# Two loads in place of one for the preceding rows of the first chunk, and a new order of the steps

## The chip, the cores and the metric

The kernel runs on one core of a Trainium2 chip. The metric is the device time of one execution in microseconds (us); lower is better. A core has TensorE (PE in the profile, its weight loads PEld), VectorE (DVE), ScalarE (ACT), GpSimd (POOL) and SyncE (SP), each with its own stream of instructions that it works off in order, and 16 DMA engines. A difference of about 0.3% between two versions is what their repeated times can tell from none.

## The reference

The input x has 8 sequences of 4160 rows of 192 numbers; each row has 8 heads with 7 taps each. The first half is a short causal attention: the taps of a head go through a softmax, and each row becomes the weighted sum of itself and the six rows ahead of it in its sequence (zeros ahead of the first).

```python
w = np.exp(weight_gen - np.max(weight_gen, axis=-1, keepdims=True))
w = w / (np.sum(w, axis=-1, keepdims=True) + 1e-09)
x_pad = zeros(B, 6, D) followed by x;  x_unf = x_pad[:, s + k]  (k = 0..6)
out = np.einsum('bshk,bskhg->bshg', w, x_unf)
```

The second half takes the 33280 rows of the result as tokens:

```python
h = x @ w_in                                   # 192 -> 1024
sm = exp(h - max(h)) / (sum(...) + 1e-09)
solu = h * sm
ln = (solu - mean) / sqrt(var + 1e-06) * g_ln
return ln @ w_out                              # 1024 -> 192
```

All of it is float32 in and out.

## The kernel before, in words

The 33280 rows are cut into 128 runs of 260 consecutive rows, one run for each partition; a sequence is 16 partitions. A tile t is row t of all 128 runs, so there are 260 tiles. They are loaded in chunks: tiles 0 to 3, 4 to 11, 12 to 19, and then 15 chunks of 16 tiles. A chunk's buffer `xt` holds the chunk's rows and the six rows ahead of them (`HALO`); there are two such buffers, and three for the taps `wt`.

For the first chunk the six rows ahead of a run are the last six rows of the run before, that is of the partition before. Line 73 loads the four rows of the chunk on all 128 partitions, line 74 clears the six rows of partition 0, and line 75 loads the last six rows of runs 0 to 126 to partitions 1 to 127. Step `x0` (line 243) then zeroes these rows where a partition begins a sequence. The second chunk takes its six rows from the first one's buffer (line 81, step `x1`); all later chunks are loaded with their six rows in four parts (`lx0` to `lx3`, line 85), the taps in one (`lw`, line 91).

The steps of a chunk, with their names in the planner: the squares of x are summed for a scale (`v00` to `v03`, ACT, line 143; then `v1` to `v5`, lines 149 to 167); the softmax of the taps is `t0` (maximum, DVE, line 107), `t1` (subtraction, POOL, line 109), `t2` (exponential, ACT, line 113), `t3` (sum, DVE, line 115), `t4` (ACT, line 118, which needs the scale from `v2`), `t5` (reciprocal, DVE, line 120) and `t6` (multiplication, POOL, line 122). Then POOL multiplies and adds for groups of four tiles (two in the first chunk): `attA` (line 178) and `attB` (lines 189 to 194); `fin` (DVE, line 469) and `dup` (ACT, line 479) finish a group.

The steps of a tile: `xT` transposes two tiles on PE (line 493), `xhi` and `xld` split them in two float16 parts (lines 501, 507), `mm1` is the first product (PE, lines 519 and 522), then `max` (DVE, 534), `exp` (ACT, 540), `solu` (DVE, 548), `sq` (ACT, 554), `hi` (ACT, 561), `lo` (DVE, 565), `tr` (a transposing DMA from SP's queue, 573), `mm2` (the second product, PE, 613), `out` (ACT, 624, which empties the accumulator `po` and so lets the next `mm2` start) and `od` (the store, 627). `f0` to `f5` are small steps on the statistics of up to four tiles (lines 588 to 604).

At the start the weights are loaded and split into two parts each (`a..`, `b..`, `c..`, `q..`, `n..`, `p..`, lines 251 to 413): raw_a and raw_b are w_in (line 207 from ACT's queue, line 208 from SP's, into the buffer named `hl`), raw_2 is w_out (line 214, into the buffer named `wide`).

What stands in which order on an engine is set in the program by a planner. `plan` lists all steps with engine, cost in ns, the steps that they wait for and an earliest time; `issue_order` plays the list through: each engine takes, among its steps whose predecessors are over, the one with the smallest key, which is the tile's number plus the step's entry in `URGENCY`. The order that comes out is the order of emission, written out under a manual schedule. The planner's times are used for nothing else; on the chip an instruction waits for what it reads, wherever it stands.

Of the kernel before, what the change touches and what calls it, by code (L numbers as in the profile page):

```python
# [26 lines left out]
def tile_kernel(ctx: ExitStack, tc: tile.TileContext, x, weight_gen, w_in, w_out, g_ln, out):  # L27
    nc = tc.nc
    P = 128
# [6 lines left out]
    HALO = K - 1  # L36
    RUN = B * S // P
    PB = P // B
# [17 lines left out]
    x_run = x.rearrange("b (q t) d -> (b q) t d", t=RUN)  # L56
# [8 lines left out]
    def load_x(c, part=0):  # L65
        t0, n = starts[c], starts[c + 1] - starts[c]
        if part == 0:
            xs[c] = io.tile([P, (TC + HALO) * D], F32, name="xt")
        xt = xs[c]
        xv = xt.rearrange("p (t d) -> p t d", d=D)  # L70
        if c == 0:

            nc.sync.dma_start(xv[:, HALO : HALO + n, :], x_run[:, :n, :])
            nc.vector.memset(xt[:1, : HALO * D], 0.0)
            nc.sync.dma_start(xv[1:, :HALO, :], x_run[: P - 1, RUN - HALO :, :])
        elif t0 < HALO:
            if part == 0:
                nc.sync.dma_start(xv[:, HALO : HALO + n, :], x_run[:, t0 : t0 + n, :])
            else:
                first = xs[0].rearrange("p (t d) -> p t d", d=D)  # L80
                nc.sync.dma_start(xv[:, :HALO, :], first[:, t0 : t0 + HALO, :])
        else:
            cuts = [(HALO + n) * k // LOADS for k in range(LOADS + 1)]
            r0, r1 = cuts[part], cuts[part + 1]
            nc.sync.dma_start(xv[:, r0:r1, :], x_run[:, t0 - HALO + r0 : t0 - HALO + r1, :])
# [146 lines left out]
    sq = const.tile([P, 8], F32, name="sq")  # L232
# [402 lines left out]
    def at_chunk(op, *args):  # L635
# [3 lines left out]
        attA=attend, attB=add_up, fin=last_sum, dup=copy_columns, xT=transpose_x,  # L639
        xhi=high_x, xld=low_x, mm1=first_product,  # L640
        max=maximum, exp=exponentials, solu=solu, sq=squares, hi=high_half, lo=low_half,
# [37 lines left out]


URGENCY = dict(
    a00=11.1, a01=-98.4, a02=25.1, a03=-179.2, a04=-48.9, a10=186.8, a11=18, a12=-184.5, a13=64.6,
    a14=-6.8, attA=76.8, attB=48.3, b0=-43.3, b1=-63.8, b2=-61.6, b3=198.8, b4=12.7, c00=62.4,
    c01=-82.8, c02=-0, c10=-111.1, c11=170.7, c12=56.5, c20=5.9, c21=34.4, c22=-3.9, c30=95.7,
    c31=-78.4, c32=-191, dup=40.3, exp=-27.1, f0=110.8, f1=-58.2, f2=-34.4, f3=-54.9, f4=15.4,
    f5=7.4, fin=13.5, hi=48.7, lo=-241.4, lw=10, lx0=53.1, lx1=133.3, lx2=75.6, lx3=108.2, max=88,
    mm1=-12.9, mm2=-6, n0=-189.5, n1=236.9, n2=-43.5, n3=-30.3, n4=153, n5=186, n6=-45.4, n7=-79.4,
    od=-11, out=-36.3, p30=-216.9, p31=16.6, p4=69.6, p5=143.5, p6=44.6, p70=154.1, p71=155.3,
    p80=127.5, p81=5.7, q00=-151, q01=12.5, q02=-55, q10=97.5, q11=-186.5, q12=108.7, q20=50,
    q21=178.6, q22=151.1, q30=-31.4, q31=-114, q32=237.3, solu=-1.8, sq=68, t0=134.4, t1=-160.3,  # L690
    t2=44.1, t3=-111, t4=-150.2, t5=-33.5, t6=245.4, tr=13.9, v00=221, v01=162, v02=94.7, v03=234.3,
    v1=-130.7, v2=160, v3=1, v4=87.6, v5=29.8, x0=-119.5, x1=-81.8, xT=-15.1, xhi=45.2, xld=182.9,
)


# [4 lines left out]
def plan(run, starts, group, stat_group, loads, parts):  # L700

    PE, DVE, ACT, SP, POOL = range(5)
    steps = []

    def add(name, t, engine, cost, *after, ready=0):
        steps.append((name, t, engine, cost, [x for x in after if x[1] >= 0], ready))

    def once(name, engine, cost, *after, ready=0):
        add(name, 0, engine, cost, *((x, 0) for x in after), ready=ready)
# [1 line left out]
    def chunk_of(t):  # L711
        return max(c for c in range(len(starts) - 1) if starts[c] <= t)

    weights = dict(a0=7000, a1=8500, b=9300, c0=13000, c1=14500, c2=15000)
    order = list(weights)
    norm_of = dict(a0="n0", a1="n1", b="n2")
    for n, part in enumerate(order):
# [28 lines left out]
    for half in "01":  # L746
        once("p7" + half, ACT, 826, "p3" + half, "p4")
        once("p8" + half, DVE, 929, "p7" + half)
    once("x0", DVE, 1200, "v00", ready=6000)
    once("x1", SP, 2500, "x0")  # L750

    def last_group(c):
# [9 lines left out]
    for c in range(len(starts) - 1):  # L762
        t, before = starts[c], starts[c - 1] if c > 1 else -1
        size = starts[c + 1] - t
        whole = size == 16
        if c > 1:
            add("lw", t, SP, 1270, last_group(c - 3))
            add("lx0", t, SP, 1540, last_group(c - 2), *parts_of(c - 2))
            for n in range(1, loads):
                add(f"lx{n}", t, SP, 1540, (f"lx{n - 1}", t))  # L770
        for part in range(4 if whole else 1):
            if c > 1:
                load = min(part + 1, loads - 1) if whole else loads - 1
                add(f"v0{part}", t, ACT, 840 if whole else 1600, (f"lx{load}", t))
            else:
                add(f"v0{part}", t, ACT, (2000, 1600)[c], ready=18000 if c else 6000)
        add("v1", t, DVE, 74, *parts_of(c), *parts_of(c - 1), ("f5", starts[c - 4] - 1 if c > 4 else -1))
        add("v2", t, ACT, 940, ("v1", t))
        add("v3", t, ACT, 480, ("v2", t), ("n6", 0))
        add("v4", t, DVE, 76, ("v3", t))  # L780
        add("v5", t, ACT, 190, ("v4", t))
        n = size * 8
        wide = 60 + 7.35 * n
        on = (DVE, POOL, ACT, DVE, ACT, DVE, POOL)
        costs = (wide, 13.4 * n, 100 + 5.9 * n, wide, 260 + n, 60 + 6.3 * n, 13.4 * n)
        for k in range(7) if c else range(4, 7):
            after = [(f"t{k - 1}", t)] if k and (c or k > 4) else []
            if k == 4:
                after.append(("v2", t))
            if k == 0 and c > 1:  # L790
                after += [("lw", t), ("t6", before)]
            add(f"t{k}", t, on[k], costs[k], *after, ready=10500 if c == 1 and not k else 0)
# [87 lines left out]
    return steps  # L880


def issue_order(steps):

    PE, DVE, ACT, SP, POOL = range(5)
    SAME, CROSS, FROM_PE = (25, 127, 143, 0, 102), 130, 200
    free = [2000, 5000, 4500, 6500, 4500]
    number = {(name, t): i for i, (name, t, *_) in enumerate(steps)}
    then, count, ready = [[] for _ in steps], [0] * len(steps), [s[5] for s in steps]
    for i, step in enumerate(steps):  # L890
        for x in step[4]:
            then[number[x]].append(i)
            count[i] += 1
    key = [round(t + URGENCY.get(name, 0), 6) for name, t, *_ in steps]
    later, now = [[] for _ in free], [[] for _ in free]
    for i, step in enumerate(steps):
        if not count[i]:
            heapq.heappush(later[step[2]], (ready[i], key[i], i))

    def gap(e, to):  # L900
        if e == to and to != SP:
            return SAME[e]
        return FROM_PE if e == PE and to != SP else CROSS

    queue = data = 0
    busy = warm = -10000
    order = []
    while True:
        able = [
            (free[e] if now[e] else max(free[e], later[e][0][0]), e)  # L910
            for e in range(len(free)) if now[e] or later[e]
        ]
        if not able:
            break
        time, e = min(able)
        while later[e] and later[e][0][0] <= time:
            _, k, i = heapq.heappop(later[e])
            heapq.heappush(now[e], (k, i))
        k, i = heapq.heappop(now[e])
        if ready[i] > time:  # L920
            heapq.heappush(later[e], (ready[i], k, i))
            continue
        name, t, _, cost, *_ = steps[i]
        order.append((name, t))
        free[e] = end = time + cost
        if e == PE:

            if name != "xT" and time - busy > 2000:
                warm = time + 3400
            if time < warm:  # L930
                free[e] = end = time + 2 * cost if time + 2 * cost < warm else (time + warm) / 2 + cost
            if name != "xT":
                busy = end
        if e == SP:
            queue = max(queue, time) + (625 if name == "tr" else 450)
            data = max(queue + 650, data) + cost
            free[e], end = time + 60, data + 950

        if name in ("sq", "lo"):
            j = number["lo" if name == "sq" else "sq", t]  # L940
            ready[j] = max(ready[j], end + CROSS)
        for j in then[i]:
            ready[j] = max(ready[j], end + gap(e, steps[j][2]))
            count[j] -= 1
            if not count[j]:
                heapq.heappush(later[steps[j][2]], (ready[j], key[j], j))
    assert len(order) == len(steps)
    return order
# [33 lines left out]
```

## Time and profile before

| | |
|---|---|
| time, median of 3 runs | 1330.26 us (1329.93 to 1333.56) |
| profiled execution | 1328.66 us, its span 1326.9 us |
| busy PE, DVE, ACT, POOL | 1212.0, 1166.0, 1179.7, 1187.2 us |
| mean granted TensorE clock | 0.993 of full speed |
| read from HBM, written | 46.19 MB, 25.56 MB |

A line of the profile names line, engine and operation, what is written and read by the program's tile names, and times in us. A wait is given as the idle time of an engine ahead of an instruction with what ended it. Matmuls are pipelined and their ends are modelled, so a busy PE is not PE at its peak; spans on POOL are rough. The profile holds one execution.

### The profile page before, as it was taken

How to read it: one execution, taken by the hardware profiler on the slowest of the kernel's cores; microseconds unless marked ns; L12 is line 12 of the kernel's file. 1: busy time of each engine (PE TensorE's matmuls, PEld its weight loads, DVE VectorE, ACT ScalarE, POOL GpSimd, SP SyncE). 2: the span in 40 equal slices, each digit the busy share in tenths (PEclk: the TensorE clock that was granted, in tenths of full speed). 3: DMA queues.
4: the chain of work that ended last, by engine and by line, in shares of the span. 5: the costliest groups of instructions: out<-in, count | busy, mean ns of one | idle time of the engine just before them, and what ended most of it. 6: DMA issues, size and time to landing. Idle time of an engine off the chain costs nothing.

```text
span 1326.9 us, 27167 instructions
## 1 busy us (share of the span) xinstructions
PE 1212.0 (91%) x10428; PEld 835.8 (63%) x10428; DVE 1166.0 (88%) x1800; ACT 1179.7 (89%) x2366; POOL 1187.2 (89%) x241
## 2 busy tenths in 40 slices
PE   0468898998999999999999999999999999999998
PEld 0245565665766666666666666666666666676666
DVE  1788898989989899998989899898989999899995
ACT  0679898999989899999999899999989999899886
POOL 0899999998999999999999999999999999999920
PEclk9979999999999999999999999999999999999999
DMA  4357779787786978688787968779697867877776
GB/s 131 108 125 167 157 132 206 144 180 151 159 183 132 204 145 185 143 171 183 135 199 149 211 129 181 159 158 193 133 206 140 191 138 157 178 143 127 128 152 129
DMA packets 565203, 210.44 MB, mean 159 GB/s; under 512 B 544337, under 2 KB 545745, under 8 KB 565072
## 3 DMA queue, kind: packets, MB, share of 16 engines
q1 hardware_dynamic: 564784, 207.64, 75.2%
q8 instruction: 82, 1.34, 0.4%
q10 hardware_dynamic: 288, 1.05, 0.2%
q14 instruction: 49, 0.40, 0.1%
HBM read 46.19 MB, written 25.56 MB: 54 GB/s over the span
## 4 chain that ended last, share of the span: by engine, by line
PE 57%; ACT 15%; DMA 11%; issue 5%; DVE 5%; POOL 4%; SPq 1%; ACTq 0%; DVEq 0%; POOLq 0%
PE po L613 25%; PE h L522 18%; DMA xt<-in_x_dram 11%; PE h L519 10%; PE pa L493 5%; ACT e L540 4%; ACT hl L561 4%; ACT e L554 4%; DVE hl L565 2%; POOL pr L178 2%; SPq L573 1%; DVE h L534 1%; ACT ot L624 1%; DVE h L548 1%; ACT x_hi L501 1%
## 5 line engine op out<-in xcount | busy, mean ns | idle before, releaser
L178 POOL TENSOR_TENSOR pr<-xt,wt 128x5376 f32<-128x5376 f32 (+1 forms) x66 | 630.9, 9558 | 3.9
L613 PE MATMUL po<-w_hl,hlT 128*128 128x192 f16 x6192 | 554.4, 246 | 33.9 <-ACT ot L624 33.9
L613 PEld LDWEIGHTS <-hlT 128*128 128x128 f16 x6240 | 523.7, 98 | 73.7 <-issue 38.9
L565 DVE SCALAR_TENSOR_TENSOR hl<-h,hl 128x1024 f16<-128x1024 f32 x260 | 315.6, 1220 | 63.9 <-ACT hl L561 32.1
L548 DVE SCALAR_TENSOR_TENSOR h<-h,row,e 128x1024 f32<-128x1024 f32 x260 | 333.2, 1282 | 36.9 <-ACT e L540 34.9
L534 DVE TENSOR_SCALAR_CACHE_REDUCE h<-h,row 128x1024 f32<-128x1024 f32 x260 | 334.4, 1286 | 11.9 <-PE h L522 10.4
L540 ACT ACTIVATE e<-h,stats 128x1024 f32<-128x1024 f32 x260 | 293.3, 1128 | 9.4 <-DVE h L534 8.1
L554 ACT ACTIVATE e<-h,stats 128x1024 f32<-128x1024 f32 x260 | 291.8, 1122 | 3.9 <-DVE hl L565 3.0
L561 ACT ACTIVATE hl<-h 128x1024 f16<-128x1024 f32 x260 | 267.4, 1028 | 28.9 <-DVE stats L585 19.4
L522 PE MATMUL h<-wa_hi,x_hi 128*128 128x512 f16 x520 | 200.7, 386 | 0.0
L522 PE MATMUL h<-wa_lo,x_hi 128*128 128x512 f16 x520 | 198.1, 381 | 0.0
L522 PE MATMUL h<-wa_hi,x_lo 128*128 128x512 f16 x520 | 198.1, 381 | 0.0
L522 PEld LDWEIGHTS <-x_hi 128*128 128x128 f16 x1040 | 80.6, 98 | 173.1 <-issue 112.2
L189 POOL TENSOR_TENSOR wide<-pr 128x2304 f32<-128x2304 f32 (+1 forms) x34 | 167.6, 4929 | 2.3
L192 POOL TENSOR_TENSOR pr<-pr 128x2304 f32<-128x2304 f32 x32 | 162.3, 5072 | 1.5
L143 ACT ACTIVATE junk<-xt 128x768 f32<-128x768 f32 (+2 forms) x63 | 56.5, 897 | 69.2 <-DMA xt<-in_x_dram 69.2
L519 PE MATMUL h<-wb_hi,x_hi 64*128 64x512 f16 x520 | 102.0, 388 | 15.5 <-ACT e L554 12.6
L624 ACT ACTIVATE ot<-po,stats 128x192 f32<-128x192 f32 x258 | 111.1, 431 | 4.0 <-PE po L613 3.6
L194 POOL TENSOR_TENSOR half<-pr 128x1536 f32<-128x1536 f32 x32 | 110.4, 3449 | 2.5
L493 PE MATMUL pa<-ident,wide 128*128 128x128 f32 x792 | 99.1, 275 | 1.6 <-DVE x_lo L507 1.1
L519 PE MATMUL h<-wb_lo,x_hi 64*128 64x512 f16 x520 | 99.7, 379 | 0.0
L519 PE MATMUL h<-wb_hi,x_lo 64*128 64x512 f16 x520 | 99.6, 378 | 0.1
(97 smaller groups left out, 1141.7 us busy)
## 6 DMA issues: line engine op xcount, KB each, us to landing
out_dram<-ot SPq DMA_DIRECT2D x65, 384.0 KB, 2.7
xt<-in_x_dram SPq DMA_DIRECT2D x30, 576.0 KB, 4.7
xt<-in_x_dram SPq DMA_DIRECT2D x30, 480.0 KB, 4.6
wt<-in_weight_gen_dram SPq DMA_DIRECT2D x15, 448.0 KB, 3.7
hlT<-hl SPq DMA_TRANSPOSE x260, 4.5
wide<-in_moe_w_out_dram SPq DMA_DIRECT2D x2, 768.0 KB, 20.6
xt<-in_x_dram SPq DMA_DIRECT2D x3, 384.0 KB, 5.2
raw_a<-in_moe_w_in_dram ACTq DMA_DIRECT2D x2, 512.0 KB, 5.9
```

Of the source, the lines that this page charges most:

```text
L178: nc.gpsimd.tensor_tensor(out=window(pr, 0, [(TG * D, K), (HG, n * H), (1, HG)]), in0=window(xt, t * D, [(D, K), (HG, n * H), (1, HG)]), i ...
L189: nc.gpsimd.tensor_tensor(out=out, in0=pr[:, :3], in1=pr[:, 3:6], op=ALU.add)
L493: nc.tensor.matmul(pa[:, n, i, :], source, ident, is_transpose=True, start=at == 0, stop=at == len(terms) - 1,)
L519: nc.tensor.matmul(h[:, fs], lhs[rows, 1, :], rhs[rows], start=n == 0, stop=False)
L522: nc.tensor.matmul(h[:, fs], lhs[:, 0, :], rhs[:, fs], start=False, stop=n == 2)
L534: nc.vector.tensor_scalar(h, h, row(t, BACK), 3.0e38, op0=ALU.mult, op1=ALU.min, accum_out=stat(t, NMAX))
L540: nc.scalar.activation(e, h_of[t], AF.Exp, bias=stat(t, NMAX), scale=-1.0, accum_out=stat(t, Z))
L548: nc.vector.scalar_tensor_tensor(out=h, in0=h, scalar=row(t, SCALE), in1=e, op0=ALU.mult, op1=ALU.mult, accum_out=stat(t, M))
L554: nc.scalar.activation(e_of.pop(t), h_of[t], AF.Square, bias=stat(t, M), scale=-float(FF), accum_out=stat(t, Q),)
L561: nc.scalar.activation(hl[:, 0, :], h_of[t], AF.Copy, scale=2.0**14)
L565: nc.vector.scalar_tensor_tensor(out=hl[:, 1, :], in0=h_of[t], scalar=2.0**14, in1=hl[:, 0, :], op0=ALU.mult, op1=ALU.subtract,)
L613: nc.tensor.matmul(po[:, :D], hlT[:, half * NJ + j, :], w2_hl[:, j, w, :], start=n == 0, stop=n == len(terms) - 1,)
```

## The change

The load of the six preceding rows of the first chunk (127 partitions) becomes two loads, of 112 and of 15 partitions, from the same place to the same place. In the planner the earliest times of the weight steps a0, a1 and b, of the first squares and of `x0`, and the cost of `x0`, are other numbers; a table `MARGIN` adds 3 or 6 us to the time between certain steps of tiles from 12 on (a name's first two letters are looked up: `lx` to `v0`, `lw` to `t0`, `lx` to `at`, and so on); and nearly all entries of `URGENCY` are new. No other instruction is added or taken away.

```diff
--- before.py
+++ after.py
@@ -72,7 +72,8 @@
 
             nc.sync.dma_start(xv[:, HALO : HALO + n, :], x_run[:, :n, :])
             nc.vector.memset(xt[:1, : HALO * D], 0.0)
-            nc.sync.dma_start(xv[1:, :HALO, :], x_run[: P - 1, RUN - HALO :, :])
+            for p0, p1 in ((1, 1 + P - PB), (1 + P - PB, P)):
+                nc.sync.dma_start(xv[p0:p1, :HALO, :], x_run[p0 - 1 : p1 - 1, RUN - HALO :, :])
         elif t0 < HALO:
             if part == 0:
                 nc.sync.dma_start(xv[:, HALO : HALO + n, :], x_run[:, t0 : t0 + n, :])
@@ -679,17 +680,18 @@
 
 
 URGENCY = dict(
-    a00=11.1, a01=-98.4, a02=25.1, a03=-179.2, a04=-48.9, a10=186.8, a11=18, a12=-184.5, a13=64.6,
-    a14=-6.8, attA=76.8, attB=48.3, b0=-43.3, b1=-63.8, b2=-61.6, b3=198.8, b4=12.7, c00=62.4,
-    c01=-82.8, c02=-0, c10=-111.1, c11=170.7, c12=56.5, c20=5.9, c21=34.4, c22=-3.9, c30=95.7,
-    c31=-78.4, c32=-191, dup=40.3, exp=-27.1, f0=110.8, f1=-58.2, f2=-34.4, f3=-54.9, f4=15.4,
-    f5=7.4, fin=13.5, hi=48.7, lo=-241.4, lw=10, lx0=53.1, lx1=133.3, lx2=75.6, lx3=108.2, max=88,
-    mm1=-12.9, mm2=-6, n0=-189.5, n1=236.9, n2=-43.5, n3=-30.3, n4=153, n5=186, n6=-45.4, n7=-79.4,
-    od=-11, out=-36.3, p30=-216.9, p31=16.6, p4=69.6, p5=143.5, p6=44.6, p70=154.1, p71=155.3,
-    p80=127.5, p81=5.7, q00=-151, q01=12.5, q02=-55, q10=97.5, q11=-186.5, q12=108.7, q20=50,
-    q21=178.6, q22=151.1, q30=-31.4, q31=-114, q32=237.3, solu=-1.8, sq=68, t0=134.4, t1=-160.3,
-    t2=44.1, t3=-111, t4=-150.2, t5=-33.5, t6=245.4, tr=13.9, v00=221, v01=162, v02=94.7, v03=234.3,
-    v1=-130.7, v2=160, v3=1, v4=87.6, v5=29.8, x0=-119.5, x1=-81.8, xT=-15.1, xhi=45.2, xld=182.9,
+    a00=-75.5, a01=196.4, a02=120, a03=-176, a04=47.5, a10=-10.6, a11=207.7, a12=103.2, a13=184.6,
+    a14=20.7, attA=-120.3, attB=-79, b0=164.4, b1=-62.4, b2=-50.4, b3=-19.9, b4=-4.1, c00=-70.9,
+    c01=120.7, c02=38.6, c10=39.6, c11=-101.6, c12=161.2, c20=147.6, c21=248.5, c22=-170.5,
+    c30=95.7, c31=-78.4, c32=-191, dup=-95.9, exp=47.3, f0=163.9, f1=-43, f2=68.5, f3=-25.1,
+    f4=-119.5, f5=-175.5, fin=178.2, hi=-75, lo=-86.8, lw=74.8, lx0=49.7, lx1=-160.2, lx2=-51.3,
+    lx3=-50.1, max=79.2, mm1=-17.5, mm2=-11.1, n0=-238.4, n1=155.8, n2=-86.8, n3=-42.6, n4=-198.3,
+    n5=149.2, n6=168.1, n7=40.5, od=-47, out=-56.3, p30=-80.9, p31=228.3, p4=51.3, p5=19.5, p6=80.1,
+    p70=225.4, p71=-108.2, p80=105.2, p81=3.6, q00=-6.6, q01=11.4, q02=150.6, q10=29.9, q11=-8.3,
+    q12=-71.5, q20=71.7, q21=44.1, q22=6.6, q30=-30.5, q31=172.3, q32=-17.3, solu=-18.3, sq=73,
+    t0=-244.2, t1=161.4, t2=-209.3, t3=175.5, t4=57.9, t5=-91.9, t6=76, tr=-50.4, v00=50.7, v01=-70,
+    v02=36.1, v03=156.4, v1=-183.3, v2=247.2, v3=131.1, v4=191.5, v5=-81.1, x0=110.7, x1=-165.6,
+    xT=-20.3, xhi=-169.3, xld=158.9,
 )
 
 
@@ -711,7 +713,7 @@
     def chunk_of(t):
         return max(c for c in range(len(starts) - 1) if starts[c] <= t)
 
-    weights = dict(a0=7000, a1=8500, b=9300, c0=13000, c1=14500, c2=15000)
+    weights = dict(a0=5700, a1=7000, b=9000, c0=13000, c1=14500, c2=15000)
     order = list(weights)
     norm_of = dict(a0="n0", a1="n1", b="n2")
     for n, part in enumerate(order):
@@ -746,7 +748,7 @@
     for half in "01":
         once("p7" + half, ACT, 826, "p3" + half, "p4")
         once("p8" + half, DVE, 929, "p7" + half)
-    once("x0", DVE, 1200, "v00", ready=6000)
+    once("x0", DVE, 820, "v00", ready=6500)
     once("x1", SP, 2500, "x0")
 
     def last_group(c):
@@ -773,7 +775,7 @@
                 load = min(part + 1, loads - 1) if whole else loads - 1
                 add(f"v0{part}", t, ACT, 840 if whole else 1600, (f"lx{load}", t))
             else:
-                add(f"v0{part}", t, ACT, (2000, 1600)[c], ready=18000 if c else 6000)
+                add(f"v0{part}", t, ACT, (2000, 1600)[c], ready=18000 if c else 6500)
         add("v1", t, DVE, 74, *parts_of(c), *parts_of(c - 1), ("f5", starts[c - 4] - 1 if c > 4 else -1))
         add("v2", t, ACT, 940, ("v1", t))
         add("v3", t, ACT, 480, ("v2", t), ("n6", 0))
@@ -880,6 +882,13 @@
     return steps
 
 
+MARGIN = {
+    ("lx", "v0"): 6000, ("lw", "t0"): 6000, ("lx", "at"): 6000, ("t0", "t1"): 6000,
+    ("t1", "t2"): 3000, ("t2", "t3"): 3000, ("t3", "t4"): 3000, ("v2", "t4"): 3000,
+    ("t5", "t6"): 6000,
+}
+
+
 def issue_order(steps):
 
     PE, DVE, ACT, SP, POOL = range(5)
@@ -897,10 +906,12 @@
         if not count[i]:
             heapq.heappush(later[step[2]], (ready[i], key[i], i))
 
-    def gap(e, to):
-        if e == to and to != SP:
-            return SAME[e]
-        return FROM_PE if e == PE and to != SP else CROSS
+    def gap(step, to):
+        e, on = step[2], to[2]
+        late = MARGIN.get((step[0][:2], to[0][:2]), 0) if to[1] > 11 else 0
+        if e == on and on != SP:
+            return SAME[e] + late
+        return (FROM_PE if e == PE and on != SP else CROSS) + late
 
     queue = data = 0
     busy = warm = -10000
@@ -940,7 +951,7 @@
             j = number["lo" if name == "sq" else "sq", t]
             ready[j] = max(ready[j], end + CROSS)
         for j in then[i]:
-            ready[j] = max(ready[j], end + gap(e, steps[j][2]))
+            ready[j] = max(ready[j], end + gap(steps[i], steps[j]))
             count[j] -= 1
             if not count[j]:
                 heapq.heappush(later[steps[j][2]], (ready[j], key[j], j))
```

## Prediction

> **What bounds the kernel now.** I read the page's chain of waits first. Its lines name TensorE (PE) for 57% of the span and a load of x for 11%, which is much for a kernel that loads ahead.
>
> ```profile
> span 1326.9 us, 27167 instructions
> PE 1212.0 (91%) x10428; PEld 835.8 (63%) x10428; DVE 1166.0 (88%) x1800; ACT 1179.7 (89%) x2366; POOL 1187.2 (89%) x241
> PE 57%; ACT 15%; DMA 11%; issue 5%; DVE 5%; POOL 4%; SPq 1%; ACTq 0%; DVEq 0%; POOLq 0%
> ```
>
> Four engines are busy for 88 to 91% of the span, so a stall of one has little room to be made up by another. Next I read the chain in order of time, and the timeline of the first 60 us, where the span is emptiest.
>
> ```profile
> 1.65 31.55 DMA xt<-in_x_dram
> ...
> 1.19 0.42 SPq L73 DMA_DIRECT2D xt<-in_x_dram  x1
> 1.65 0.32 SPq L75 DMA_DIRECT2D xt<-in_x_dram  x1
> 2.02 13.62 SPq L208 DMA_DIRECT2D hl<-in_moe_w_in_dram  x2
> 33.31 1.80 ACT L143 ACTIVATE junk<-xt 128x1920 f32<-128x1920 f32 x1 [31.30 <-DMA xt<-in_x_dram]
> 35.24 0.16 DVE L149 TENSOR_REDUCE row<-squares_x 128x1 f32<-128x8 f32 x1 [27.41 <-ACT junk L143]
> 38.40 0.57 POOL L122 TENSOR_TENSOR wt<-wt,wy 128x224 f32<-128x224 f32 x1 [32.17 <-DMA xt<-in_x_dram]
> 42.20 0.67 ACT L270 ACTIVATE size<-wide 128x512 f32<-128x512 f32 x1 [3.73 <-DVE h L274]
> 57.94 0.61 PE L519 MATMUL h<-wb_hi,x_hi 64*128 64x512 f16 x2
> ```
>
> The load of line 75 (the preceding rows of the first chunk) is issued at 1.65 us and is back at 33.20 us. ACT's first instruction on data waits for it, DVE's line 149 waits for ACT, POOL's line 122 for what follows from that: the three engines stand still together. The second column of these rows is a duration; the brackets hold the idle time before the row. The first product of the main loop starts at 57.94 us. The same stretch by windows (columns: window, its length, busy time and count of PE, PEld, DVE, ACT, POOL, clock, DMA share, GB/s) and the sizes of the loads (KB each, median us from issue to landing) tell why:
>
> ```profile
> 2.00:4.00 2.00, 0.00 (x0) 0.00 (x0) 0.29 (x4) 0.01 (x1) 0.00 (x0) 1.00 0.82 210
> 4.00:6.00 2.00, 0.00 (x0) 0.00 (x0) 0.71 (x2) 0.00 (x0) 0.59 (x2) 1.00 0.98 354
> 6.00:8.00 2.00, 0.00 (x0) 0.00 (x0) 1.76 (x3) 0.00 (x0) 0.23 (x1) 1.00 0.55 221
> 8.00:10.00 2.00, 0.00 (x0) 0.00 (x0) 0.00 (x0) 0.00 (x0) 0.00 (x0) 1.00 0.06 25
> 12.00:15.00 3.00, 0.00 (x0) 0.00 (x0) 0.00 (x0) 0.00 (x0) 0.00 (x0) 1.00 0.06 26
> ...
> xt<-in_x_dram SPq DMA_DIRECT2D x30, 576.0 KB, 4.7
> wide<-in_moe_w_out_dram SPq DMA_DIRECT2D x2, 768.0 KB, 20.6
> raw_a<-in_moe_w_in_dram ACTq DMA_DIRECT2D x2, 512.0 KB, 5.9
> xt<-in_x_dram SPq DMA_DIRECT2D x1, 571.5 KB
> hl<-in_moe_w_in_dram SPq DMA_DIRECT2D x2, 256.0 KB, 25.6
> ```
>
> From 8 to 15 us the share is 0.06, one sixteenth of the core's 16 DMA engines, at 25 GB/s. The only load that can be under way then is the one of 571.5 KB on 127 partitions; it runs on one engine, and SP's next issue (line 208, 13.62 us) and all weights (20.6 and 25.6 us to landing) stand behind it. A load of the same size on 128 partitions lands in 4.7 us.
>
> By the Trainium skill ("DMA: Bandwidth & Descriptors", section "Why a DMA increments its semaphore by 16 and not by 1") a DMA uses the largest number of engines up to 16 that divides its slowest dimension, 127 giving 1; the share of 0.06 agrees. By the same rule 112 partitions would use 16 engines and 15 would use 15, which no row of before shows.
>
> Then the steady part. The waits between 200 and 1200 us (us in total, times, longest):
>
> ```profile
> ACT junk L143 <- DMA xt<-in_x_dram: 34.8, 25, 4.0
> PE po L613 <- ACT ot L624: 23.3, 13, 2.9
> PE pa L493 <- ACT a L479: 7.5, 12, 0.6
> POOL wt L122 <- DVE wy L120: 28.5, 12, 3.7
> ...
> 762.07 0.84 ACT L143 ACTIVATE junk<-xt 128x768 f32<-128x768 f32 x1 [1.53 <-DMA xt<-in_x_dram]
> 765.38 0.43 ACT L624 ACTIVATE ot<-po,stats 128x192 f32<-128x192 f32 x1
> 765.86 2.14 PE L613 MATMUL po<-w_hl,hlT 128*128 128x192 f16 x24 [1.64 <-ACT ot L624]
> 780.39 1.76 POOL L122 TENSOR_TENSOR wt<-wt,wy 128x896 f32<-128x896 f32 x1 [2.22 <-DVE wy L120]
> 742.00:818.00 76.00, 73.63 (x642) 50.85 (x641) 69.90 (x108) 71.20 (x143) 72.99 (x15) 1.00 0.79 167
> 1200.00:1300.00 100.00, 99.85 (x876) 69.67 (x876) 91.42 (x140) 88.97 (x170) 67.36 (x12) 1.00 0.73 134
> ```
>
> ACT waits 1.53 us for a quarter of a chunk's x; 2.5 us later in its order comes the line 624 that frees the accumulator, and PE, which needs it, stands 1.64 us. In the same chunk POOL stands 2.22 us for the reciprocal of the taps. The window of 76 us (about one chunk of 16 tiles) has PE busy for 73.63 and POOL for 72.99 us; with its wait POOL is at 75.2, so both are near the bound, and the gap is what these waits cost. The window from 1200 us shows that PE can be busy for 99.85 of 100 us.
>
> **The change, part by part.** *The split load.* One issue of 0.32 us is added on SP (row of line 75); what stands behind it is line 208, which no longer waits 13 us, so it costs nothing. When do both parts land? Bytes of the four transfers that start first: 112 KB of weights for the taps, 384 KB of x (128 partitions x 4 rows x 768 B), 1024 KB of raw_a and 571.5 KB, together 2.14 MB. The windows move 0.42 MB from 2 to 4 us and 0.71 MB from 4 to 6; the remaining 1.0 MB at 354 GB/s end at 8.8 us. Early bound: issue plus 4.7 us, 6.4. Late bound: nothing here shows a load on 15 partitions; on one engine its 69 KB take 2.8 us at 25 GB/s, 11.6. I take 8.8, since the rows of 128 partitions fill the engines to 0.98 and 112 is the bulk. ACT starts at 8.8 in place of 33.3: 24.5 us earlier (21.7 to 26.9).
>
> Is anything else late then? The weights end at 4.47 MB in all (2.14, then 524 KB of raw_b, 229 KB of taps, 1.57 MB of w_out): at 354 GB/s that is 15.5 us, and the first use of w_out (line 270 on wide, 42.20) would come at 17.7, so the stall is hidden by 2 us. At 221 GB/s they end at 21, 3.4 us late, and the gain falls to 21. From 35.24 us on DVE is nearly without gaps until the first product, and its work there is unchanged, so the whole opening moves by the same 24.5 us, the first product to about 33.4.
>
> By the Trainium skill (the same page, section "Rules for kernel authors") transfers to disjoint halves of the partitions are not worth splitting, because both go over the same 16 engines and serialise. By that rule line 75 would land as before and this term would be 0; it is taken up as a rival.
>
> *Constants and costs of the planner* (due times of the weights, of the first squares, the cost of x0) and *the margins* add no instruction and no wait. They and the new urgencies change only the order in which the same instructions stand on the five engines. A margin holds back the reader of a load in the plan by 6 us, so it stands later in its engine's order. Lateness in the trace is at most 4.0 us for ACT and 3.7 us for POOL, both below the 6 us that the margins for lx to v0 and for t5 to t6 allow. The loads start about a chunk (76 us) ahead of their attention, so holding line 143 back costs no wait by itself. Gain: at most what PE loses to it, 23.3 + 7.5 = 30.8 us. I take half, 15.5 us. More is held up by POOL, which after its wait goes still needs 72.99 us and its gaps between 15 instructions, and by ACT, whose other waits a new order shuffles. Below nothing: the order is new for every step, loads and transposes on SP too (a load ahead of a transpose delays hlT and then PE's line 613), so I allow a loss of 4 us. The opening itself, between 58 and 200 us, has 23 us of PE waits:
>
> ```profile
> PE h L519 <- ACT e L554: 12.1, 2, 11.5
> PE po L613 <- ACT ot L624: 8.2, 5, 3.0
> PE pa L493 <- DVE x_lo L507: 2.8, 2, 1.8
> ```
>
> I price its new order at 0, with 6 us (a quarter) either way: while PE waits 11.5 us here, POOL is without gaps on the next group, which PE needs anyhow.
>
> *Sum* against the profiled execution, 1328.66 us (span 1326.9 and 1.8 around it): 1328.66 - 24.5 - 15.5 = 1288.7. The median of the runs, 1330.26, is 1.6 above that execution, so 1290.3; I forecast **1290 us**.
>
> **Rivals.** (1) *Opening only*: the new order leaves as many stalls as the old, others in their place. For: every engine is at 92% or more of the chunk window, and an order that is new throughout has new odd spots. Against: the listed waits are exactly of the edges that get margins. 1330.3 - 24.5 = 1306. (2) *All goes*: the waits of 30.8 us and a quarter of the opening's go as well: 1330.3 - 24.5 - 30.8 - 6 = 1269. For: PE at 99.85% from 1200 us, where no loads are left. Against: POOL's 72.99 us. (3) *Part of the opening is lost again* to w_out landing late and to new waits of 4 to 15 us: 1310 to 1326. (4) *The split does not shorten the load*, either because both parts pass through one engine or because the time is the memory's: then only the order counts, 1330.3 - 15.5 = 1315. Against: a share of 0.98 at 354 GB/s from the same memory between 4 and 6 us. This is the case that the skill's rule on disjoint halves stands for. (5) *Slower*: the new order puts a wait for a small statistic ahead of the high half on ACT in each group of four tiles. It is there now in half of them:
>
> ```profile
> ACT hl L561 <- DVE stats L585: 15.7, 26, 0.9
> ```
>
> In all 65 groups at its longest, 0.9 us, it makes 58.5 us in place of 15.7: 1330.3 - 24.5 + 42.8 = 1349. It turns the sign from about 0.44 us for each group that reach PE (28.5 us over 65, the opening's gain and 4 us). Against it speaks that no such wait reaches PE in the present rows.
>
> **How the numbers follow.** Chances: forecast (both gains, 1275 to 1303) 0.60; (1) 0.15; (2) 0.12; (3) 0.06; (4) 0.02; (5) 0.03; a wash within 4 us, by several of these, 0.02. The range reaches from 1266 (all bounds of the gains: 26.9 + 30.8 + 6) to 1314 (21 from the opening, 4 lost in the order); it leaves out about 0.15. The bound for a difference is 0.3%, 4 us: faster 0.95, same 0.02, slower 0.03.
>
> **What would show it.** Right: ACT's first line 143 starts between 6.4 and 11.6 us; the window from 8 to 15 us has a DMA share far over 0.06; line 208 is issued in under 2 us; the first line 519 stands near 33 us; from 200 to 1200 us ACT's waits for x are below 10 us, POOL's line 122 below 10 us, and PE waits some 15 us less in all. Wrong on the split: one part still lands after 20 us. Wrong on the order: ACT's and POOL's waits go, and PE's stay near 30 us under other names; then POOL's or DVE's work, not the loads, sets the chunk.

## The result, and the profile after

The changed kernel takes 1270.97 us (median of 4, 1270.70 to 1271.80); the kernel before, timed beside it, 1331.12 us. The ratio is 0.9547 (95% interval 0.9530 to 0.9563): 60 us less. The forecast was 1290 us in a range of 1266 to 1314.

The page of the changed kernel (span, busy times, chain by engine, and the group of the second product) and its windows, with the columns as before:

```profile
span 1269.1 us, 27095 instructions
PE 1209.8 (95%) x10428; PEld 834.5 (66%) x10428; DVE 1169.4 (92%) x1800; ACT 1178.8 (93%) x2366; POOL 1187.3 (94%) x241
POOL 28%; PE 23%; ACT 22%; DVE 14%; issue 9%; DMA 2%; SPq 0%; POOLq 0%; DVEq 0%; ACTq 0%
L614 PE MATMUL po<-w_hl,hlT 128*128 128x192 f16 x6192 | 556.2, 247 | 6.7 <-ACT ot L625 3.8
```

```profile
2.00:4.00 2.00, 0.00 (x0) 0.00 (x0) 0.29 (x4) 0.01 (x1) 0.00 (x0) 1.00 0.81 194
4.00:6.00 2.00, 0.00 (x0) 0.00 (x0) 0.80 (x2) 0.41 (x1) 0.44 (x1) 1.00 0.98 353
6.00:8.00 2.00, 0.00 (x0) 0.00 (x0) 1.67 (x3) 0.25 (x1) 0.39 (x2) 1.00 1.08 361
8.00:10.00 2.00, 0.00 (x0) 0.00 (x0) 0.81 (x3) 0.00 (x0) 0.00 (x0) 1.00 1.01 228
10.00:12.00 2.00, 0.00 (x0) 0.00 (x0) 1.35 (x3) 0.97 (x1) 0.00 (x0) 1.00 1.03 237
...
200.00:1200.00 1000.00, 996.96 (x8681) 688.09 (x8680) 947.91 (x1445) 957.82 (x1912) 989.11 (x190) 1.00 0.82 168
```

Its opening in the timeline:

```profile
1.66 1.38 SPq L76 DMA_DIRECT2D xt<-in_x_dram  x2
3.08 1.29 SPq L209 DMA_DIRECT2D hl<-in_moe_w_in_dram  x2
11.03 1.80 ACT L144 ACTIVATE junk<-xt 128x1920 f32<-128x1920 f32 x1 [4.78 <-DMA xt<-in_x_dram]
15.72 0.58 POOL L123 TENSOR_TENSOR wt<-wt,wy 128x224 f32<-128x224 f32 x1
16.83 0.65 ACT L271 ACTIVATE size<-wide 128x512 f32<-128x512 f32 x1
32.38 0.61 PE L520 MATMUL h<-wb_hi,x_hi 64*128 64x512 f16 x2
```

All lines from 76 on stand one further down than before. The same amount of work is done in 57.8 us less span; PE's busy time differs by 2.2 us, so a change of PE's clock is not what saved it. The first product comes 25.6 us earlier (32.38 against 57.94 us); the other 32.2 us are saved behind it. There the window from 200 to 1200 us tells most. For the kernel before it reads:

```profile
200.00:1200.00 1000.00, 966.80 (x8381) 666.71 (x8380) 915.38 (x1403) 932.88 (x1860) 960.97 (x185) 1.00 0.80 166
```

PE is idle for 3 of 1000 us where it was idle for 33. No wait of ACT for x and none of POOL for the reciprocals is left in that stretch, and of PE's waits 0.9 us:

```profile
PE h L520 <- DVE hl L566: 0.6, 1, 0.6
PE po L614 <- ACT ot L625: 0.3, 1, 0.3
```

### The profile page after: what moved, and what is told of

It reads as the page before. It is cut to its first block, busy times and chain, and to the rows that moved or that the text cites. A ratio compares the mean times of both kernels' runs of the same rounds, so it can differ in the third digit from the quotient of the medians.

```text
span 1269.1 us, 27095 instructions
## 1 busy us (share of the span) xinstructions
PE 1209.8 (95%) x10428; PEld 834.5 (66%) x10428; DVE 1169.4 (92%) x1800; ACT 1178.8 (93%) x2366; POOL 1187.3 (94%) x241
## 4 chain that ended last, share of the span: by engine, by line
POOL 28%; PE 23%; ACT 22%; DVE 14%; issue 9%; DMA 2%; SPq 0%; POOLq 0%; DVEq 0%; ACTq 0%
POOL pr L179 15%; PE po L614 10%; ACT e L541 7%; PE h L523 7%; POOL wide L190 6%; ACT hl L562 5%; ACT e L555 4%; DVE h L549 4%; DVE hl L566 4%; PE h L520 4%; DVE h L535 3%; POOL pr L193 2%; POOL wide L191 2%; DMA xt<-in_x_dram 2%; ACT ot L625 2%
## 5 line engine op out<-in xcount | busy, mean ns | idle before, releaser
L520 PE MATMUL h<-wb_hi,x_hi 64*128 64x512 f16 x520 | 101.8, 388 | 15.5 <-DVE hl L566 12.2
L494 PEld LDWEIGHTS pa<-ident,wide 128*128 128x128 f32 x792 | 90.8, 142 | 16.3 <-issue 5.7
```

The lines of the kernel that those rows point to most:

```text
L494: nc.tensor.matmul(pa[:, n, i, :], source, ident, is_transpose=True, start=at == 0, stop=at == len(terms) - 1,)
L520: nc.tensor.matmul(h[:, fs], lhs[rows, 1, :], rhs[rows], start=n == 0, stop=False)
```

## The experiments

**The two halves of the change apart.** First the split alone, in the old order.

```diff
-            nc.sync.dma_start(xv[1:, :HALO, :], x_run[: P - 1, RUN - HALO :, :])
+            for p0, p1 in ((1, 1 + P - PB), (1 + P - PB, P)):
+                nc.sync.dma_start(xv[p0:p1, :HALO, :], x_run[p0 - 1 : p1 - 1, RUN - HALO :, :])
```

> The kernel before with nothing but the load split in 112 and 15 partitions; the old order stays. Theory (the opening's stall and the later waits add up): the preceding rows land at about 11 us in place of 33.2, as in the changed kernel, and the whole program moves forward by the same 22 us: 1331 - 22 = 1309 us (1306 to 1312); ACT's waits for x (34.8 us from 200 to 1200 us), POOL's for the taps' reciprocal (28.5) and PE's (30.8) stay as they are. Rival (the gains overlap, the opening's stall is partly made up later): 1315 to 1325 us.

It took 1313.39 us against 1333.12 beside it, 0.9844 (0.9825 to 0.9863): 19.7 us. From its timeline:

```profile
10.83 1.80 ACT L144 ACTIVATE junk<-xt 128x1920 f32<-128x1920 f32 x1 [8.82 <-DMA xt<-in_x_dram]
35.45 0.61 PE L520 MATMUL h<-wb_hi,x_hi 64*128 64x512 f16 x2
```

The time is a little above the expected 1306 to 1312 us: the first product is 22.5 us earlier, and some 3 us of it are not in the total. In its profile ACT waits somewhat longer for the later loads (38.7 us from 200 to 1200 us; 34.8 in the profile of before), but a kernel below that has the old opening shows 37.3 as well, so where the 3 us went stays open. Then the new order with the one load put back:

```diff
 # the changed kernel, with
-            for p0, p1 in ((1, 1 + P - PB), (1 + P - PB, P)):
...
+            nc.sync.dma_start(xv[1:, :HALO, :], x_run[: P - 1, RUN - HALO :, :])
```

> The changed kernel with the one load of 127 partitions put back; the new order stays. Theory: only the opening is late again, 1271 + 22 to 25 = 1293 to 1296 us, and from 200 to 1200 us PE still waits under 3 us. Rival (the new order needs the early start, and its waits come back with the late one): above 1305 us.

It took 1294.03 us, 0.9702 (0.9686 to 0.9719) of the kernel before: 39.1 us. From 200 to 1200 us PE waits 1.1 us, about as little as with the split (0.9). So the halves add up: 19.7 and 39.1 us are 58.8 of the 60.2. Nearly two thirds are the order's.

**Why the split helps.** The number of loads stays two, and one partition changes sides:

```diff
-            for p0, p1 in ((1, 1 + P - PB), (1 + P - PB, P)):
+            for p0, p1 in ((1, 114), (114, P)):
```

> The changed kernel with the cut moved by one partition: 113 and 14 in place of 112 and 15. Theory (the number of engines follows from the divisors of the partition count, and 113 has none up to 16): the larger part runs on one engine, 520 KB at 25 GB/s, a DMA share near 0.06 once the other loads are through, ACT's first line on data starts at 28 to 31 us, and the time is 1288 to 1294 us. Rival (what helps is that there are two loads, or a shorter one): about 1271 us.

It took 1290.59 us (0.9677), 3.4 us less than with the one load of 127. Its windows and timeline show the load of 113 partitions as the only one under way, on one of 16 engines, with SP's next issue behind it:

```profile
8.00:10.00 2.00, 0.00 (x0) 0.00 (x0) 1.81 (x5) 0.00 (x0) 0.00 (x0) 1.00 0.06 25
10.00:12.00 2.00, 0.00 (x0) 0.00 (x0) 0.35 (x1) 0.00 (x0) 0.00 (x0) 1.00 0.06 25
```

```profile
1.65 10.33 SPq L76 DMA_DIRECT2D xt<-in_x_dram  x2
30.87 1.80 ACT L144 ACTIVATE junk<-xt 128x1920 f32<-128x1920 f32 x1 [24.43 <-DMA xt<-in_x_dram]
```

Two loads, the longer of them a ninth shorter than before, are worth these 3.4 us together; the rest is the count of 112. This agrees with the rule of the Trainium skill on divisors ("DMA: Bandwidth & Descriptors", section "Why a DMA increments its semaphore by 16 and not by 1"), by which 113, a prime, gets one engine. The same page's advice against splitting a transfer by partitions (section "Rules for kernel authors") does not hold for a count such as 127: its reason is that both halves use the engines that the whole would use, and here the whole used one.

**Which wait set the steady part.** Three kernels keep the old order on every engine and are to take a wait away by giving the waiting instruction older data.

```diff
-            xv = xs[c].rearrange("p (t d) -> p t d", d=D)              # norm_x, step 0
+            xv = xs[c - 1 if c > 3 else c].rearrange("p (t d) -> p t d", d=D)
```

> The kernel before, where from the fifth chunk on the squares (line 143) are taken of the chunk before, whose x is long there; the squares of the chunk's own x are left out, so the scale belongs to other rows. Order and instructions stay. This takes ACT's wait for the loads away in the old order. Theory (ACT's wait sets PE's): ACT's 34.8 us go, most of PE's 30.8 us between 200 and 1200 us with them, 1331 - 22 to 30 = 1301 to 1309 us. Rival (POOL's wait for the taps' reciprocal holds the chunk as it is): 1325 us or more.

```diff
+            y = taps[c - 1 if c > 3 else c][1]                         # softmax_taps, step 6
             nc.gpsimd.tensor_tensor(
                 out=w3, in0=w3, in1=y.unsqueeze(2).broadcast_to(wide), op=ALU.mult
```

> The kernel before, where from the fifth chunk on POOL multiplies the taps by the reciprocals of the chunk before; the chunk's own reciprocals are computed and left out there. This takes POOL's 28.5 us of waits away in the old order. Theory (PE's waits come from ACT, POOL runs ahead of its users): 1328 to 1332 us. Rival (POOL is the bound of the chunk): 1305 to 1315 us.

> Both of the above in the kernel before: the squares and the reciprocals of the chunk before, from the fifth chunk on. Theory (these two waits are all that the new order saved after the opening): PE waits under 5 us from 200 to 1200 us, 1331 - 28 to 33 = 1298 to 1303 us. Rival (the new order saves by other changes too): 1308 us or more.

The squares alone: 1292.89 us against 1333.55, 0.9695 (0.9672 to 0.9718), 40.7 us. The reciprocals alone: 1333.00 us, 1.0012 (0.9984 to 1.0040), nothing. Both: 1293.80 us, 0.9700, no more than the squares alone. Both kernels with the squares ready came out below their expected 1301 to 1309 and 1298 to 1303 us, which had been worked out from PE's listed waits. With the squares ready, PE's window and its waits are nearly those of the changed kernel, in the old order:

```profile
200.00:1200.00 1000.00, 995.72 (x8680) 691.07 (x8679) 946.73 (x1448) 961.05 (x1917) 989.10 (x190) 1.00 0.82 170
```

```profile
PE h L519 <- ACT e L554: 2.4, 12, 0.2
PE h L519 <- DVE hl L565: 0.5, 1, 0.5
```

POOL is busy for 989 us there although its own waits were left in place: they, too, went with ACT's. Where only the reciprocals were older, ACT's and PE's waits stayed, and PE's window is the old one:

```profile
200.00:1200.00 1000.00, 964.03 (x8354) 664.75 (x8352) 913.18 (x1401) 930.69 (x1855) 965.73 (x185) 1.00 0.80 166
```

```profile
ACT junk L144 <- DMA xt<-in_x_dram: 37.3, 25, 4.5
PE po L614 <- ACT ot L625: 25.8, 13, 3.4
POOL wt L109 <- DVE wm L107: 23.8, 11, 3.0
```

The last row shows that this edit did not do what was expected of it. Of POOL's 28.5 us of waits 23.8 only moved, from the reciprocal (line 122) to the maximum of the taps (line 109), which also comes from DVE. So this kernel does not price POOL's waits. The answer comes from the kernel with the squares ready: there ACT's wait for x alone was taken away, and POOL's and PE's went with it.

So ACT's wait for x is the cause. Whether it reaches the end straight from ACT to PE or also by way of POOL is not separated. The group of line 144 in the kernel with the older reciprocals, and what ended the idle time ahead of it (us, times):

```profile
DMA xt<-in_x_dram: 72.1, 29
```

Without the opening's one wait of 31.6 us that is 40.5 us, and the gain was 40.7. The profile of before has 37.9 us of these waits, and its span is 36.1 us longer than that with the squares ready. Within 2 us, a microsecond of this wait cost a microsecond of the time. If that is all, the old order with the split and the squares ready must reach the changed kernel's time.

> The kernel before with the load split in 112 and 15 partitions and, from the fifth chunk on, the squares of the chunk before (those of the chunk's own x are left out); the old order stays. Theory (the load of the opening and ACT's wait for the later loads are all that the change saved): 1333 - 20 - 41 = 1272 us (1269 to 1276), with PE waiting under 5 us from 200 to 1200 us. Rival (the new order saves something else besides): 1280 us or more.

It took 1270.87 us, 0.9531 (0.9511 to 0.9551). The changed kernel's ratio is 0.9547 (0.9530 to 0.9563). For the time the new order is worth what the removal of this one wait is worth in the old order, and nothing that can be measured beside it.

**What in the new order removes it.** Four kernels make the order anew from other margins.

```diff
-        late = MARGIN.get((step[0][:2], to[0][:2]), 0) if to[1] > 11 else 0
+        late = 0
```

> The changed kernel with every margin at zero; the new urgencies stay, so the order is made anew without them. Theory (the margins keep the readers behind their loads): ACT waits for x 20 to 40 us again from 175 to 1175 us or POOL 15 to 30 us for the reciprocals, and the time is 1290 to 1305 us. Rival (the new urgencies do it by themselves): 1270 to 1276 us, with ACT's waits for x under 5 us.

> The changed kernel with every margin longer by a sixth, 7 and 3.5 us; every lateness that 6 us covered stays covered, but the order is made anew. Theory (the waits that are covered set the time, the rest of the order is not delicate): 1270 to 1276 us, ACT's waits for x under 5 us. Rival (any new order under these urgencies has stalls of its own, and what the kernel without margins lost says little of the margins): 1285 us or more with ACT's waits for x still under 5 us.

```diff
 MARGIN = {
-    ("lx", "v0"): 6000, ("lw", "t0"): 6000, ("lx", "at"): 6000, ("t0", "t1"): 6000,
...
+    ("lx", "v0"): 6000, ("lw", "t0"): 6000, ("lx", "at"): 6000,
 }
```

> The changed kernel with the three margins behind loads alone (lx to v0, lw to t0, lx to attA, 6 us); those within the taps' softmax are zero. Theory (only ACT's wait for x counts, POOL's does not reach PE): ACT's waits for x stay under 5 us, POOL waits 15 to 35 us again, and the time is 1271 to 1278 us. Rival (the margins of the taps are needed, or the order is delicate): 1290 us or more.

> The kernel before with the split load and the table of margins; urgencies, due times and costs stay the old ones, so the order is made anew from them. Theory (the margins do it, the new urgencies are secondary): ACT's waits for x under 5 us, 1271 to 1282 us. Rival (the urgencies have to fit the margins): the waits for x go and others come, 1290 to 1320 us.

| kernel | time, us | ratio to before | ACT's waits for x, 200 to 1200 us | PE's waits, same stretch |
|---|---|---|---|---|
| the changed one | 1270.97 | 0.9547 | none listed | 0.9 |
| margins 7 and 3.5 us | 1297.07 | 0.9726 | none listed | 24.6 |
| margins of the loads alone | 1294.50 | 0.9708 | none listed | 22.3 |
| old urgencies, split, margins | 1308.96 | 0.9817 | none listed | 35.4 |
| no margins | 1329.48 | 0.9974 | 31.8 | 46.4 |

Without margins ACT's waits for x are back, as the theory had it, but the time rose by 58 us, twice what it gave, and missed the expected 1290 to 1305 us. POOL's waits for the reciprocals are back there too (34.0 us). With margins of any of the three kinds ACT's waits for x are gone and the time is still 23 to 38 us above the changed kernel's. PE then waits for others, here with the old urgencies:

```profile
PE po L614 <- ACT ot L625: 21.1, 25, 1.4
PE h L520 <- DVE hl L566: 7.0, 9, 2.7
PE h L520 <- ACT e L555: 6.3, 7, 2.3
PE pa L494 <- DVE x_lo L508: 1.0, 3, 0.4
```

These are waits between the steps of a tile, which no margin covers: ACT and DVE wait for each other in turn, and the accumulator is emptied late. POOL is not late there: its last instruction starts at 1212.8 us with the old urgencies and at 1212.1 us in the changed kernel, while the spans are 1306.7 and 1269.1 us. So the rivals named in the last three expectations hold. The margin does take the wait for the load away wherever it was tried; whether the order that results has other stalls is decided by the urgencies, and of the tables tried under those of the change only its own gives an order without them: margins longer by a sixth lose 26 us. What the margins of the taps alone are worth in time can't be read from the kernel without them, because its whole order is another. They are not needed to spare POOL its waits: with the margins of the loads alone 15 to 35 us of these were expected, and none is listed from 200 to 1200 us.

**A version beyond.** The opening still waits 4.78 us for the preceding rows, behind 1 MB of raw_a from ACT's queue. The second half of it was put behind them:

```diff
-        nc.scalar.dma_start(raw_a[:, f * FF : (f + 1) * FF], w_in[:P, f * FF : (f + 1) * FF])
+    nc.scalar.dma_start(raw_a[:, :FF], w_in[:P, :FF])
+    nc.sync.dma_start(raw_a[:, FF:], w_in[:P, FF:])
```

> The changed kernel with the second half of raw_a (512 KB) issued from SP's queue behind the preceding rows, not from ACT's queue ahead of them. Theory (the rows are late by the bytes ahead of them, and POOL's start sets the end): they land 1.5 to 2.5 us earlier than 11.0 us, POOL's first multiplication starts as much earlier, and the time is 1268.5 to 1270 us. Rival (DVE's work on the weights sets the opening): within 1 us of 1271; if the second half is late for DVE, up to 1273 us.

It took 1270.45 us, 0.9526 (0.9512 to 0.9540): not told apart from the change. From its timeline:

```profile
9.27 1.80 ACT L144 ACTIVATE junk<-xt 128x1920 f32<-128x1920 f32 x1 [3.09 <-DMA xt<-in_x_dram]
10.94 0.69 DVE L263 TENSOR_SCALAR h<-raw_a 128x512 int32<-128x512 int32 x1 [3.03 <-DMA raw_a<-in_moe_w_in_dram]
13.16 0.15 DVE L150 TENSOR_REDUCE row<-squares_x 128x1 f32<-128x8 f32 x1
15.58 0.58 POOL L123 TENSOR_TENSOR wt<-wt,wy 128x224 f32<-128x224 f32 x1
```

The rows come 1.8 us earlier, but DVE, in whose order a conversion of raw_a stands ahead of the sum of the squares, now waits 3.03 us for the half that was moved (1.46 us before), and POOL starts 0.14 us earlier. The wait changed engines; the rival on DVE's work was right.

## Why the prediction was right or wrong

*The load on one engine.* Right, and shown by the cut at 113. The rows were to land at 8.8 us (6.4 to 11.6) and landed at 11.0. Two steps were off. 354 GB/s was carried on to the end, while the windows from 8 to 12 us moved 228 and 237 GB/s with all engines taken. And 2.14 MB were counted as moved before the rows are there, while the windows up to 11 us add up to 2.5 MB: part of the loads issued behind was moved ahead of the last rows. The term, 24.5 us, is 22.3 at ACT's first line and 25.6 at the first product; the new order of the opening made up 3.1 us (32.38 against 35.45 us with the split in the old order). In the total the split is worth 19.7 us in the old order.

*w_out hidden.* Right: its first use (line 271 on wide) runs at 16.83 us with no wait ahead of it, and SP issues the loads of raw_b in 1.29 us where they took 13.62.

*The order of the opening*, priced at 0 with 6 us either way: held. The 3.1 us above do not show in the total: the old order with the split and the squares ready starts its first product at 36.03 us and takes the same time.

*The term of the margins*, 15.5 us, is where the prediction fell short: it measured 39.1 us. So 1271 us lies in the stated range, near its lower end, but outside the 1275 to 1303 us that were given 0.60; the mechanism was right, and this term was put at less than half of what it measured. Two steps failed. "I take half" rested on POOL, which "after its wait goes still needs 72.99 us and its gaps", and on ACT's other waits. But the window quoted there holds 72.99 us of POOL's work and 73.63 of PE's in 76, which left room for more than half: afterwards POOL ran 989 of 1000 us and PE 997. And "at most what PE loses to it, 30.8 us" was no bound. It added up PE's listed waits between 200 and 1200 us, while ACT waits for x from the opening up to 1142 us, and PE's idle time in the window was 33.2 us. The row from which to price it was ACT's own, in the groups of the kernel before:

```profile
L143 ACT ACTIVATE junk<-xt 128x768 f32<-128x768 f32 (+2 forms) x63 | 56.5, 897 | 69.2 <-DMA xt<-in_x_dram 69.2
```

Less the opening's 31.3 us these are 37.9 us, and the kernels with the squares ready show that they were to be taken one for one; the pair of 1.53 us on ACT and 1.64 us on PE in the prediction's rows already has that rate.

*What the margins do.* They do take the late loads out of ACT's way, as said. That the same instructions in another order cost nothing else was assumed in pricing, but for the 4 us allowed, and holds for this order alone; three others with margins lose 23 to 38 us. The warning that "a new order shuffles" ACT's other waits was right even here: from 200 to 1200 us they rose from 25.7 to 37.9 us. In this order PE hardly waited for ACT; in the three others it did.

*Rivals.* "All goes", 1269 us, given 0.12, is nearest to what happened, though POOL did not stand against it and its extra gain in the opening was not needed. "Opening only" is out as a whole, and its price, 1306, is near what the split alone gives, 1313. "The split does not shorten the load" and "slower" are out.

## What to carry to other kernels

Look at the DMA share where nothing else runs: a share of one sixteenth was a load on one engine here, and its partition count is the first thing to try; 112 and 15 in place of 127 was worth 20 us, 113 and 14 only 3.4. Where four engines are each busy for 90%, look for the wait that comes first, here ACT's for a load, and price it by its own idle time, not by what is listed on the engines behind it; not every idle microsecond counts so, as ACT's other waits rose without a loss. Prove it by giving the waiting instruction older data: that keeps the order and costs one line. Then read the waits again, since the stall may only have moved to the neighbouring instruction. An order written out by a planner is good for the numbers that it was made with; after any change to them the waits have to be read again, since a margin that removes one stall moves all the others.

## What the runs showed of the hardware that was not expected

With all 16 engines taken (shares of 1.01 and 1.03), the loads of the opening moved 228 to 237 GB/s between 8 and 12 us and 353 between 4 and 6 us. Which of the loads then under way is the slower one was not tried. And a load at a share of one sixteenth held back the issue of those behind it: SP's two issues took 10.33 us with 113 partitions and 1.38 with 112.
